# Gate and value products of the last two token groups in seven half-size products instead of eight

## The chip, the cores and the metric

The kernel runs on one core of one Trainium2 chip. The metric is the device time of one execution in microseconds (us); three runs of the kernel before gave 333.61, 334.01 and 334.57 us, median 334.01 us. The profile is one more execution of the same kernel, and it took 332.81 us.

## What is computed

Attention with a sliding window of 128 and a linear distance bias feeds a gated feed-forward block.

```python
scores = np.where(mask, scale * q @ k.T + bias, -1e9)      # 8 batches, 8 heads, 576 x 576, 64 deep
attn = softmax(scores) @ v                                  # 8 x 8 x 576 x 64
x = attn.transpose(0, 2, 1, 3).reshape(4608, 512)           # tokens x d_model
g = x @ w_gate                                              # 512 -> 1536
gelu = 0.5 * g * (1.0 + erf(g / sqrt(2)))
out = (gelu * (x @ w_val)) @ w_out                          # 1536 -> 512
```

## The kernel before, in words

**Groups and batches.** The 4608 tokens are worked through in nine groups `g` of 512. Attention of batch `g + 2` (scores, exponentials, masks, sums, products with v) is woven into the feed-forward work of group `g`, so that the last batch's attention is done in group 6 and groups 7 and 8 hold feed-forward work alone. The order of instructions on each engine is the order of the code; nothing is rescheduled. Each engine works through its own queue in that order and waits on semaphores for the others.

**Gate and value.** `gate_val(g, f)` (L631) makes one block `f` of 128 of the 1536 hidden columns: four matmuls of 128 x 512 into one PSUM bank for the gate and four into another for the value (L648; the contraction over 512 goes in four steps `c`). ScalarE then writes the GELU of the gate to `gelu` (L655), and VectorE multiplies the value bank with it into `hT` (L656). Twelve blocks make a group. PSUM has eight banks, handed out in turn by `bank()`, so matmuls run up to four blocks ahead of VectorE.

**Output products.** Groups 2 to 8 make the product with `w_out` in seven half-size products in place of eight (a Strassen-Winograd scheme): `combine_left` (L718) makes four sums of `hT` on VectorE, in three pieces at f = 7, 9 and 11, `product` (L739) makes the seven products in matmuls of 256 columns (L749), and `gather_out` (L756) copies and adds them from PSUM into `osb`. `out_products` (L1014) sets their order. For groups 7 and 8 it is the short list at L1018, for group 6 the branch at L1031, which also holds the last attention products.

**Around group 6.** At its beginning VectorE still has the last masks of batch 7 (L235) and the partial sums `T` of its weights to make (`add`, L385 to L395, run at f = 1 from `put_off`). They feed `sums4`, matmuls on `T` that stand behind block f = 4 in TensorE's queue (L438).

**Pool.** GpSimd issues the loads of q, k, v and the weights, sets a few tiles to zero, and has nothing to do after the load of v for batch 7 in group 5.

**Tiles that are free at the end.** `Ps[0]` (weights of even batches), `emask` (decay masks), `T`, `qT`, `kT` and `qs[0]` have no reader left in groups 7 and 8.

Of the kernel before, what the change touches and what calls it, by code (L numbers as in the profile page):

```python
# [7 lines left out]
FP32 = mybir.dt.float32  # L8
BF16 = mybir.dt.bfloat16
AF = mybir.ActivationFunctionType  # L10
ALU = mybir.AluOpType
# [10 lines left out]
COLUMNS0 = ((0, 192, 384), (None, None, 512, 704, 512))  # L22

RING = 2048

PRODUCTS = range(2, 9)

# [7 lines left out]
def kernel(  # L35
# [34 lines left out]
    def bank():  # L70
        return psum.tile([128, 512], FP32, name="ps")
# [51 lines left out]
    def load_v(b, js=range(5)):  # L123
        load(vb[b % 2], v, b, js, 64)
# [506 lines left out]
    def gate_val(g, f, lo=0, hi=512, later=None):  # L631
        if g not in hid:
            hid[g] = h_pool.tile([128, NF, 512], BF16, name="hT")
        t0 = 512 * g % RING
        n = hi - lo

        if n > 256 or lo >= 384:
            pg, pv = bank()[:, 0:n], bank()[:, 0:n]
            order = [(w, ps, c, c == 0) for w, ps in ((wg, pg), (wv, pv)) for c in range(4)]
        else:  # L640
            ps = bank()
            pg, pv = ps[:, 0:n], ps[:, n:2 * n]
            order = [(w, ps, c, w is wg and c == 0)
                     for cs in ((0, 1), (2, 3)) for w, ps in ((wg, pg), (wv, pv)) for c in cs]
        cols = ((0, 256), (256, 512)) if (g, f) in HALVED else ((0, n),)
        for w, ps, c, begins in order:
            for a, e in cols:
                nc.tensor.matmul(  # L648
                    out=ps[:, a:e], lhsT=w[:, c, 128 * f:128 * (f + 1)], rhs=xT[:, c, t0 + lo + a:t0 + lo + e],
                    start=begins and a == 0, stop=(c == 3),  # L650
                    skip_group_check=n <= 256 and lo < 384 or len(cols) > 1)

        def act():
            gl = g_pool.tile([128, 512], BF16, name="gelu")
            nc.scalar.activation(out=gl[:, 0:n], in_=pg, func=AF.Gelu)  # L655
            nc.vector.tensor_tensor(out=hid[g][:, f, lo:hi], in0=pv, in1=gl[:, 0:n],  # L656
                                    op=ALU.mult)

        if later is None:
            act()  # L660
        else:
            later.append(act)
# [10 lines left out]
    def store():  # L673
        for args in stores:
            nc.sync.dma_start(**args)
        stores.clear()
# [41 lines left out]
    def combine_left(g, lo, hi):  # L718
        x, ns = halves(g), slice(lo, hi)
        a11, a12, a21, a22 = (x[:, ns, e, h, :] for h in (0, 1) for e in (0, 1))  # L720
        s1, s2, s4 = (left[:, n, ns, :] for n in range(3))
        for to, a, b, op in ((s1, a21, a22, ALU.add), (s2, s1, a11, ALU.subtract),
                             (s4, a12, s2, ALU.subtract), (a21, a11, a21, ALU.subtract)):
            nc.vector.tensor_tensor(out=to, in0=a, in1=b, op=op)
# [14 lines left out]
    def product(g, n, a):  # L739
# [6 lines left out]
        for i in range(NF // 2):  # L746
# [2 lines left out]
            nc.tensor.matmul(out=made[g, a, into], lhsT=lhsT, rhs=rhs, start=first and i == 0,  # L749
                             stop=i == NF // 2 - 1, skip_group_check=True)  # L750

    def finished(g, t, osb):
        r0 = 512 * g + 128 * t
        stores.append(dict(out=out[r0:r0 + 128, :], in_=osb))
# [259 lines left out]
    def out_products(g):  # L1014
        b = g + 2
        O = lambda what, a, copy=act: gather_out(g, a, what, copy)
        P = lambda n, a: product(g, n, a)
        if b > B:  # L1018
            for n, after in ((1, ("p1",)), (2, ()), (6, ("u2", "c11")), (5, ("p5",)), (7, ("c22",)), (4, ("c21",)),
                             (3, ("c12",))):  # L1020
                for a in (0, 1):
                    P(n, a)
                    for what in after:
                        O(what, a)
                store()
            return
        P(1, 0)
        P(2, 0)
        O("p1", 0)
        urgent = 512 * (g + 2) - S * (b - 1)  # L1030
        if b == B:  # L1031
            P(6, 0)
            O("u2", 0)
            O("c11", 0)
            P(5, 0)
            O("p5", 0)
            P(7, 0)
            O("c22", 0)
            scale = values(b - 1, later=True)
            P(4, 0)  # L1040
            O("c21", 0)
            P(3, 0)
            scale[0]()
            scale[1]()
            O("c12", 0)
            P(1, 1)
            O("p1", 1)
            store()
            P(2, 1)
            for do in scale[2:]:  # L1050
                do()
            O("c11", 1)
            P(6, 1)
            O("u2", 1)
            P(5, 1)
            O("p5", 1)
            P(7, 1)
            O("c22", 1)
            P(3, 1)
            O("c12", 1)  # L1060
            P(4, 1)
            O("c21", 1)
            return
        exp_table()
        O("c11", 0)
        later = []
        scores2(b, 0, later)
        A = later[0]
        P(6, 0)
        O("u2", 0, dve)  # L1070
        P(5, 0)
        for n in (0, 1, 3):
            A[n]()
        O("p5", 0)
        A[2]()
        P(7, 0)
        O("c22", 0)
        A[4]()
        for n in (5, 6, 7):
            A[n]()  # L1080
        P(1, 1)
        P(4, 0)
        P(3, 0)
        O("p1", 1)
        O("c21", 0)
        O("c12", 0)
        A[8]()
        A[9]()
        scores2(b, 2, later)
        A = later[1]  # L1090
        P(2, 1)
        P(6, 1)
        O("u2", 1, dve)
        O("c11", 1)
        add(b, 0, None, (0,))
        P(5, 1)
        for n in (0, 1, 3, 5):
            A[n]()
        O("p5", 1)
        A[2]()  # L1100
        P(7, 1)
        O("c22", 1)
        A[4]()
        for n in (6, 7):
            A[n]()
        store()
        scale, more = values(b - 1, urgent=urgent)
        for do in scale:
            do()
        P(4, 1)  # L1110
        P(3, 1)
        O("c21", 1)
        for do in more:
            do()
        O("c12", 1)
        A[8]()
        A[9]()
        add(b, 0, None, (2, 1))
        put_off.append(lambda: add(b, 2))
# [3 lines left out]
    for g in range(NG):  # L1123
        if 1 <= g < B - 2:
            transposes_dma(3 if g == 1 else g + 2)
        if g == 1:

            nc.gpsimd.tensor_copy(out=mark, in_=kT[1][0:1, 0, 512:514])
            load_qk(4)
            load_v(3)  # L1130
        for f in range(9 if g == 0 else 0, NF):
            gate_val(g, f)
            if f == 1:
                for do in put_off:
                    do()
                put_off.clear()
                store()
            if g == 1 and f in (3, 5, 7, 9):
                combine_right(f // 2 - 1)
            if g in PRODUCTS and f in (7, 9, 11):  # L1140
                combine_left(g, *{7: (0, 3), 9: (3, 5), 11: (5, 6)}[f])
            if g == 2 and f == 2:
                add(3, 2, act, (1,))
            if g == 0 and f == 10:
                masks_of_last_blocks(0, 8)
            if g == 0 and f == 9:
                for c in range(4):
                    for w in (0, 1):
                        transpose(1, w, c, (act, dve)[w])
            if 2 <= g < B - 1:  # L1150
                if f == (5 if g == 2 else 4):
                    sums4(g + 1)
                if f == (7 if g == 2 else 6):
                    gather(g + 1)
                if f == (9 if g == 2 else 8):
                    spread_dma(g + 1)
                if f == 9 and g + 2 < B:

                    nc.gpsimd.tensor_copy(out=mark, in_=hid[g][0:1, f, 0:2])  # L1159
                    if g + 3 < B:  # L1160
                        load_qk(g + 3)
                    load_v(g + 2)
        if g == 0:
            nc.gpsimd.memset(Ps[0][:, :, 0:64], 0.0)
            for t in (qs[1], ks[1]):
                nc.gpsimd.memset(t[64:128, 4, :], 0.0)
        if g in PRODUCTS:
            out_products(g)
        else:
            for item in steps(g):  # L1170
                if isinstance(item, int):
                    out_part(g, item)
                else:
                    RUN[item[0]](*item[1:])
            store()
        if g == 0:
            load_v(2)
            nc.gpsimd.tensor_copy(out=mark, in_=qT[0][0:1, 0, 512:514])
            load_qk(3)
# [30 lines left out]
```

## Time and profile before

| | us |
|---|---|
| median of three runs | 334.01 |
| profiled execution | 332.81 |
| its span, first to last instruction | 331.0 |
| TensorE busy | 321.9 (97%) |
| VectorE busy | 244.2 (74%) |
| ScalarE busy | 174.7 (53%) |
| GpSimd busy | 109.5 (33%) |

The 1.8 us between the profiled execution and its span lie outside the instructions. In the profile PE is TensorE's matmuls, PEld its weight loads, DVE is VectorE, ACT ScalarE, POOL GpSimd. The granted TensorE clock is 1.0 throughout. A group of instructions is named by line, engine, operation and tiles, with its count, its busy time in us, the mean of one in ns, and the idle time of the engine just before it.

### The profile page before, as it was taken

The numbers are of one execution on the slowest core, as the hardware profiler recorded it, in microseconds if no ns is written. First come the engines' busy times: TensorE is split into PE (matmuls) and PEld (weight loads), VectorE is DVE, ScalarE is ACT, GpSimd is POOL, SyncE is SP. The second block draws the span as 40 slices with busy tenths as digits, with TensorE's granted clock in tenths as the row PEclk, the third lists the DMA queues.
The fourth block names the chain that finished last, engine by engine and source line by source line (L and its number), as shares of the span: only waits on it lengthen the run. The fifth ranks groups of instructions, "written<-read, shape, count | busy, mean of one in ns | idle before, by whom it ended". The sixth has DMA issues, their size and how long they took to land.

```text
span 331.0 us, 8767 instructions
## 1 busy us (share of the span) xinstructions
PE 321.9 (97%) x3513; PEld 192.7 (58%) x3544; DVE 244.2 (74%) x505; ACT 174.7 (53%) x341; POOL 109.5 (33%) x144
## 2 busy tenths in 40 slices
PE   8999999999999999999999999999999999999995
PEld 6566655544654477446844685458544854584474
DVE  8888776465779978978798879896997643933662
ACT  8974687537798276336643484338423233323331
POOL 5964789190292095007700690040000000000000
PEclk9999999999999999999999999999999999999999
DMA  8999999999799999949994999489105210011003
GB/s 218 170 197 189 204 168 183 131 220 146 158 155 142 142 199 193 152 115 200 185 144 111 180 192 152 129 159 119 69 1 135 73 69 0 2 61 68 0 0 128
DMA packets 149629, 43.53 MB, mean 131 GB/s; under 512 B 133556, under 2 KB 142420, under 8 KB 149588
## 3 DMA queue, kind: packets, MB, share of 16 engines
q0 software_dynamic: 107456, 18.10, 75.6%
q1 hardware_dynamic: 38960, 18.69, 26.0%
q10 hardware_dynamic: 3172, 6.19, 8.0%
q8 instruction: 27, 0.44, 0.6%
q14 instruction: 14, 0.11, 0.1%
HBM read 43.65 MB, written 9.53 MB: 161 GB/s over the span
## 4 chain that ended last, share of the span: by engine, by line
PE 93%; ACT 2%; DMA 1%; issue 1%; DVE 1%; SPq 0%
PE ps L648 56%; PE ps L749 19%; PE ps L502 5%; PE ps L685 5%; PE ps L301 2%; ACT P L232 2%; PE ps L705 2%; PE ps L219 1%; DMA qs<-in_q_dram 1%; PE ps L438 1%; PE ps L157 1%; ACT osb L769 0%; SPq L807 0%; DVE qT L165 0%; ACT rb L599 0%
## 5 line engine op out<-in xcount | busy, mean ns | idle before, releaser
L655 ACT ACTIVATE gelu<-ps 128x512 bf16<-128x512 f32 (+3 forms) x117 | 65.6, 564 | 107.4 <-PE ps L648 98.8
L648 PE MATMUL ps<-xT,wv 128*128 128x512 bf16 (+4 forms) x467 | 112.3, 361 | 0.3
L648 PE MATMUL ps<-xT,wg 128*128 128x512 bf16 (+4 forms) x454 | 110.9, 360 | 1.1 <-issue 0.3
L656 DVE TENSOR_TENSOR hT<-ps,gelu 128x512 bf16<-128x512 f32 (+3 forms) x117 | 73.3, 644 | 41.6 <-PE ps L648 36.5
L648 PEld LDWEIGHTS <-wv 128*128 128x128 bf16 x472 | 45.0, 98 | 48.8 <-DVE xT L556 0.6
L648 PEld LDWEIGHTS <-wg 128*128 128x128 bf16 x472 | 44.4, 98 | 46.4
L232 ACT ACTIVATE P<-ps 128x512 bf16<-128x512 f32 (+1 forms) x108 | 52.3, 575 | 4.0 <-PE ps L301 2.1
L235 DVE TENSOR_TENSOR P<-P,emask 128x768 bf16<-128x768 bf16 x60 | 32.0, 554 | 8.1 <-ACT P L232 6.3
L749 PEld LDWEIGHTS <-hT 128*128 128x128 bf16 x336 | 32.0, 97 | 6.4
L115 POOL DMA_DIRECT2D vb<-in_v_dram x40 | 33.9, 887 | 2.9 <-DMA wo<-in_moe_w_out_dram 1.0
L1159 POOL COPY mark<-hT 1x2 bf16<-1x2 bf16 x4 | 1.5, 366 | 77.8 <-DVE hT L656 77.8
L749 PEld LDWEIGHTS <-left 128*128 128x128 bf16 x252 | 24.3, 98 | 3.0
L115 POOL DMA_DIRECT2D qs<-in_q_dram x30 | 25.2, 857 | 1.8 <-issue 0.9
L115 POOL DMA_DIRECT2D ks<-in_k_dram x30 | 25.4, 889 | 0.3 <-DMA qs<-in_q_dram 0.3
L749 PE MATMUL ps<-right,hT 128*128 128x256 bf16 x168 | 22.1, 272 | 0.0
L749 PE MATMUL ps<-wo,hT 128*128 128x256 bf16 x168 | 21.0, 273 | 0.0
L749 PE MATMUL ps<-right,left 128*128 128x256 bf16 x168 | 20.3, 273 | 0.0
L502 PE MATMUL ps<-P,vb 64*64 64x192 bf16 (+2 forms) x752 | 18.5, 221 | 1.4 <-ACT P L232 0.7
L502 PEld LDWEIGHTS <-vb 64*64 64x64 bf16 x752 | 15.0, 107 | 4.3 <-issue 3.3
L685 PE MATMUL ps<-wo,hT 128*128 128x512 bf16 x66 | 15.9, 380 | 0.7 <-issue 0.6
L773 ACT COPY osb<-ps 128x256 f32<-128x256 f32 x14 | 5.6, 399 | 16.0 <-PE ps L749 16.0
L385 DVE TENSOR_TENSOR T<-P 64x1024 bf16<-64x1024 bf16 x20 | 13.7, 683 | 0.3
(111 smaller groups left out, 313.7 us busy)
## 6 DMA issues: line engine op xcount, KB each, us to landing
out_dram<-osb SPq DMA_DIRECT2D x36, 256.0 KB
rb<-rd ACTq DMA_DIRECT2D x10, 576.0 KB
vb<-in_v_dram POOLq DMA_DIRECT2D x32, 128.0 KB, 6.7
qs<-in_q_dram POOLq DMA_DIRECT2D x24, 128.0 KB, 5.1
ks<-in_k_dram POOLq DMA_DIRECT2D x24, 128.0 KB, 6.1
wo<-in_moe_w_out_dram POOLq DMA_DIRECT2D x4, 384.0 KB, 12.1
wg<-in_moe_w_gate_dram POOLq DMA_DIRECT2D x5, 256.0 KB, 8.6
wv<-in_moe_w_val_dram POOLq DMA_DIRECT2D x5, 256.0 KB, 9.6
```

Source lines behind the costliest of these rows:

```text
L115: nc.gpsimd.dma_start(out=t[at:at + n, j, :].rearrange("p (h d) -> p h d", h=H), in_=src[b][:, 128 * j:128 * j + n, :].rearrange("h p d -> ...
L232: nc.scalar.activation(out=dst, in_=src, func=AF.Exp, scale=0.125)
L235: nc.vector.tensor_tensor(out=dst, in0=dst, in1=m, op=ALU.mult)
L301: mm = nc.tensor.matmul(out=ps[64 * x:64 * x + 64, col:col + w], lhsT=keys(b, c, m)[half, :], rhs=qT[b % 2][half, c, q0:q0 + w], start=Tru ...
L385: nc.vector.tensor_tensor(out=to[half, :, x:x + 7:2], in0=P[half, :, 0:10:3], in1=P[half, :, 1:11:3], op=ALU.add)
L502: mm = nc.tensor.matmul(out=out, lhsT=lhsT, rhs=prob(b)[half, c, i, col:col + q1 - q0], start=all(t[2] != u for t in todo[:n]), stop=True, ...
L648: nc.tensor.matmul(out=ps[:, a:e], lhsT=w[:, c, 128 * f:128 * (f + 1)], rhs=xT[:, c, t0 + lo + a:t0 + lo + e], start=begins and a == 0, st ...
L655: nc.scalar.activation(out=gl[:, 0:n], in_=pg, func=AF.Gelu)
L656: nc.vector.tensor_tensor(out=hid[g][:, f, lo:hi], in0=pv, in1=gl[:, 0:n], op=ALU.mult)
L685: nc.tensor.matmul(out=acc[g], lhsT=hid[g][:, f, 128 * t:128 * (t + 1)], rhs=wo[:, f, :], start=(f == 0), stop=(f == NF - 1))
L705: nc.tensor.matmul(out=acc[g, t], lhsT=hid[g][:, f, 128 * t:128 * (t + 1)], rhs=wo[:, f, :], start=(f == 0), stop=(f == NF - 1))
L749: nc.tensor.matmul(out=made[g, a, into], lhsT=lhsT, rhs=rhs, start=first and i == 0, stop=i == NF // 2 - 1, skip_group_check=True)
```

## The change

In groups 7 and 8 the blocks f = 0 to 3 and f = 6 to 9 are no longer made by `gate_val`. `gate_quad` makes four blocks at a time. It takes gate and value weights as the two rows of a 2 x 2 block matrix and the two halves of the contraction as its columns; the other factor has the two halves of the contraction as rows and the two halves of 256 tokens as columns. The product of the two comes in seven products, each of eight matmuls of 256 columns (two output banks `u`, two blocks `e`, two steps `c`). Blocks 4, 5, 10 and 11 stay with `gate_val`.

The sums that go into it are new. `combine_weights` makes four sums of weights for each of the two places, 16 additions of 128 x 512 on GpSimd, at the beginning of group 6, into `Ps[0]` and `emask`. `combine_x` makes four sums of tokens of a group, 128 x 512 each, on VectorE, into `T`: for group 7 at the end of group 6, for group 8 behind block 4 of group 7. What comes out of it is new too: P1, U = P1 + P6 and P5 are copied from PSUM to float32 tiles (`wide`), five copies on ScalarE and one on VectorE; six additions on VectorE add a PSUM bank to them; four GELUs read those tiles; VectorE multiplies the first half of the tokens (two operations), GpSimd the second half (two). The pieces of `combine_left` move from f = 7, 9, 11 to f = 4, 5, 10, 11.

```diff
+    def combine_weights():
+        for f0, at in QUADS.items():
+            for c in (0, 1):
...
+                for to, a, b, op in ((s1, v1, v2, ALU.add), (s2, s1, g1, ALU.subtract),
+                                     (s3, g1, v1, ALU.subtract), (s4, g2, s2, ALU.subtract)):
+                    nc.gpsimd.tensor_tensor(out=to, in0=a, in1=b, op=op)
...
+        factors = {1: (g1, b11), 2: (g2, b21), 3: (s4, b22), 4: (v2, t4), 5: (s1, t1), 6: (s2, t2), 7: (s3, t3)}
...
+        P(1)
+        for u in (0, 1):
+            copy(out=P1[u], in_=banks["x", u])
+        P(2)
+        for u in (0, 1):
+            add_to("z", P1, u)
+        gelu(0, P1, 0)
+        P(6)
+        copy(out=U[0], in_=banks["x", 0])
+        dve(out=U[1], in_=banks["x", 1])
+        P(5)
+        for u in (0, 1):
+            copy(out=P5[u], in_=banks["y", u])
+        gelu(0, P1, 1)
+        P(7)
+        for u in (0, 1):
+            add_to("x", P5, u)
+        P(3)
+        for u in (0, 1):
+            add_to("y", U, u)
+            gelu(1, U, u)
+        P(4)
+        for u in (0, 1):
+            nc.vector.tensor_tensor(out=hidden(u, 0), in0=both(banks["x", u]), in1=both(gelus[u]), op=ALU.mult)
+            nc.gpsimd.tensor_tensor(out=hidden(u, 1), in0=both(P5[u]), in1=both(gelus[2 + u]), op=ALU.mult)
...
+            combine_x(g + 1)                      # end of out_products, group 6
...
+        if g == B - 2:
+            combine_weights()
+        if g >= B - 1:
+            for f in range(NF):
+                if f in QUADS:
+                    gate_quad(g, f)
+                elif not any(f0 < f < f0 + 4 for f0 in QUADS):
+                    gate_val(g, f)
+                if f == 4:
+                    store()
+                    combine_left(g, 0, 2)
+                    if g + 1 < NG:
+                        combine_x(g + 1)
+                if f in (5, 10, 11):
+                    combine_left(g, *{5: (2, 3), 10: (3, 5), 11: (5, 6)}[f])
+            out_products(g)
+            continue
```

Two places of the queues, in the order of instructions. A name in brackets is an engine whose semaphore the instruction waits for; DVE in an instruction of DVE is an earlier result of its own. First VectorE's queue before, from the first block of group 7 on: `hT<-ps,gelu` is the multiplication of a block, `left` and `hT<-hT` are `combine_left`.

```order
L656 TENSOR_TENSOR hT<-ps,gelu 128x512 [waits DVE_49,PE_49,Activation_49]
L656 TENSOR_TENSOR hT<-ps,gelu 128x512 [waits PE_49,Activation_49] x7
L724 TENSOR_TENSOR left<-hT 128x768 [waits DVE_49]
L724 TENSOR_TENSOR left<-left,hT 128x768 [waits DVE_49]
L724 TENSOR_TENSOR left<-hT,left 128x768 [waits DVE_49]
L724 TENSOR_TENSOR hT<-hT 128x3x256
L656 TENSOR_TENSOR hT<-ps,gelu 128x512 [waits PE_49,Activation_49] x2
```

The same queue after, in the first four blocks of group 7, behind the four operations of `combine_x`: `qT_99` holds P1, `kT_101` U and `qT_100` P5; `qs_95` holds the GELUs.

```order
L816 TENSOR_TENSOR qT_99<-ps,qT_99 128x512 [waits PE_49,Activation_49] x2
L836 COPY kT_101<-ps 128x512 [waits PE_49]
L816 TENSOR_TENSOR qT_100<-ps,qT_100 128x512 [waits PE_49,Activation_49] x2
L816 TENSOR_TENSOR kT_101<-ps,kT_101 128x512 [waits PE_49,Activation_49]
L816 TENSOR_TENSOR kT_101<-ps,kT_101 128x512 [waits DVE_49,PE_49]
L850 TENSOR_TENSOR hT<-ps,qs_95 128x2x256 [waits DMASW1_49,PE_49]
L850 TENSOR_TENSOR hT<-ps,qs_95 128x2x256 [waits DMASW2_49,PE_49,Activation_49]
L658 TENSOR_TENSOR hT<-ps,gelu 128x512 [waits PE_49,Activation_49]
L726 TENSOR_TENSOR left<-hT 128x512 [waits Pool_49]
L726 TENSOR_TENSOR left<-left,hT 128x512 [waits DVE_49]
L726 TENSOR_TENSOR left<-hT,left 128x512 [waits DVE_49]
L726 TENSOR_TENSOR hT<-hT 128x2x256
```

Four blocks took four operations of VectorE and take nine, and the first piece of `combine_left` now waits for Pool. Behind it in the queue stand the four operations of `combine_x` for group 8, the multiplication of block 5, and the next piece of `combine_left`.

The second place is the end of Pool's queue. Before, it ends with the load of v for batch 7 in group 5:

```order
L1159 COPY mark<-hT 1x2
L115 DMA vb_104<-in_v_dram 128x8x64 x4
L115 DMA vb_104<-in_v_dram 64x8x64
L1205 UNCONDITIONAL_BRANCH
L1205 ISA
```

After, the sums of weights stand behind that load (`P_105` is `Ps[0]`):

```order
L1278 COPY mark<-hT 1x2
L117 DMA vb_104<-in_v_dram 128x8x64 x4
L117 DMA vb_104<-in_v_dram 64x8x64
L768 TENSOR_TENSOR P_105<-wv 128x512
L768 TENSOR_TENSOR P_105<-P_105,wg 128x512
L768 TENSOR_TENSOR P_105<-wg,wv 128x512
L768 TENSOR_TENSOR emask<-wg,P_105 128x512
L768 TENSOR_TENSOR P_105<-wv 128x512
L768 TENSOR_TENSOR P_105<-P_105,wg 128x512
L768 TENSOR_TENSOR P_105<-wg,wv 128x512
L768 TENSOR_TENSOR emask<-wg,P_105 128x512
```

Eight more of the same follow, and then eight multiplications into `hT`, two for each four blocks. The first sum waits for the last reader of `Ps[0]`, the products of batch 6 with v in group 5.

More of the change, by code (lines that the diff above doesn't have):

```diff
@@ L24 @@
 RING = 2048
+QUADS = {0: 0, 6: 512}
 PRODUCTS = range(2, 9)
@@ L750, in product, with flat_of @@
                              stop=i == NF // 2 - 1, skip_group_check=True)
+    def flat_of(t):
+        return t.rearrange("p a x -> p (a x)")
+    sums_w = [flat_of(t)[:, lo:lo + 2048].rearrange("p (c f) -> p c f", c=2)
+              for t, lo in ((Ps[0], 0), (Ps[0], 2048), (Ps[0], 4096), (emask, 0))]
+    def combine_weights():
+        for f0, at in QUADS.items():
+            for c in (0, 1):
+                g1, g2, v1, v2 = (w[:, x, 128 * f0:128 * f0 + 512]
+                                  for w, x in ((wg, c), (wg, 2 + c), (wv, c), (wv, 2 + c)))
+                s1, s2, s3, s4 = (t[:, c, at:at + 512] for t in sums_w)
+                for to, a, b, op in ((s1, v1, v2, ALU.add), (s2, s1, g1, ALU.subtract),
+                                     (s3, g1, v1, ALU.subtract), (s4, g2, s2, ALU.subtract)):
+                    nc.gpsimd.tensor_tensor(out=to, in0=a, in1=b, op=op)
@@ new lines, in sums_x, with tokens, combine_x @@
+    def sums_x(g):
+        return [flat_of(T)[:, 2048 * (g % 2) + 512 * n:2048 * (g % 2) + 512 * n + 512].rearrange(
+            "p (c x) -> p c x", c=2) for n in range(4)]
+    def tokens(g):
+        t0 = 512 * g % RING
+        return [xT[:, c:c + 2, t0 + x:t0 + x + 256] for c in (0, 2) for x in (0, 256)]
+    def combine_x(g):
+        b11, b12, b21, b22 = tokens(g)
+        t1, t2, t3, t4 = sums_x(g)
+        for to, a, b, op in ((t1, b12, b11, ALU.subtract), (t2, b22, t1, ALU.subtract),
+                             (t3, b22, b12, ALU.subtract), (t4, b21, t2, ALU.subtract)):
+            nc.vector.tensor_tensor(out=to, in0=a, in1=b, op=op)
@@ new lines, with gate_quad, P, add_to @@
+    wide = [flat_of(t)[:, 1024 * i:1024 * i + 1024].bitcast(FP32)
+            for t in (qT[0], kT[0], qT[1]) for i in (0, 1)]
+    gelus = [flat_of(qs[0])[:, 512 * i:512 * i + 512] for i in range(4)]
+    def gate_quad(g, f0):
+        if g not in hid:
+            hid[g] = h_pool.tile([128, NF, 512], BF16, name="hT")
+        b11, b12, b21, b22 = tokens(g)
+        t1, t2, t3, t4 = sums_x(g)
+        s1, s2, s3, s4 = (t[:, :, QUADS[f0]:QUADS[f0] + 512] for t in sums_w)
+        g1, g2, v1, v2 = (w[:, c:c + 2, 128 * f0:128 * f0 + 512] for w in (wg, wv) for c in (0, 2))
+        factors = {1: (g1, b11), 2: (g2, b21), 3: (s4, b22), 4: (v2, t4), 5: (s1, t1), 6: (s2, t2), 7: (s3, t3)}
+        banks = {}
+        def P(n):
+            w, x = factors[n]
+            for u in (0, 1):
+                if n in (1, 2, 5):
+                    banks[INTO[n], u] = bank()
+                ps = banks[INTO[n], u]
+                for e in (0, 1):
+                    at = 256 * u + 128 * e
+                    for c in (0, 1):
+                        nc.tensor.matmul(
+                            out=ps[:, 256 * e:256 * e + 256], lhsT=w[:, c, at:at + 128], rhs=x[:, c, :],
+                            start=n in (1, 2, 5) and e == 0 and c == 0, stop=c == 1, skip_group_check=True)
+        copy, dve = nc.scalar.copy, nc.vector.tensor_copy
+        P1, U, P5 = wide[0:2], wide[2:4], wide[4:6]
+        def add_to(n, to, u):
+            nc.vector.tensor_tensor(out=to[u], in0=banks[n, u], in1=to[u], op=ALU.add)
+        def gelu(what, frm, u):
+            nc.scalar.activation(out=gelus[2 * what + u], in_=frm[u], func=AF.Gelu)
+        def both(x):
+            return x.rearrange("p (e x) -> p e x", e=2)
+        def hidden(u, half):
+            return hid[g][:, f0 + 2 * u:f0 + 2 * u + 2, 256 * half:256 * half + 256]
+        P(1)
[20 more added lines that the diff above has]
+        P(4)
+        for u in (0, 1):
+            nc.vector.tensor_tensor(out=hidden(u, 0), in0=both(banks["x", u]), in1=both(gelus[u]), op=ALU.mult)
+            nc.gpsimd.tensor_tensor(out=hidden(u, 1), in0=both(P5[u]), in1=both(gelus[2 + u]), op=ALU.mult)
```

## Prediction

> **What bounds the kernel now.** First the page: how much of the span TensorE is busy.
>
> ```profile
> span 331.0 us, 8767 instructions
> PE 321.9 (97%) x3513; PEld 192.7 (58%) x3544; DVE 244.2 (74%) x505; ACT 174.7 (53%) x341; POOL 109.5 (33%) x144
> ```
>
> Then the chain of waits over the end of the program, columns start, us, what. It begins here with group 8.
>
> ```profile
> 297.34 10.74 PE ps L648 x49
> 308.07 0.05 issue
> 308.13 9.88 PE ps L648 x45
> 318.00 9.26 PE ps L749 x84
> 327.26 0.02 issue
> 327.29 0.42 DVE osb L776
> ```
>
> Nothing but matmuls stands in it: whatever shortens TensorE's queue in groups 7 and 8 shortens the time, and whatever makes it wait lengthens it. Group 8's gate and value matmuls run from 297.34 to 318.00, 20.66 us for 12 x 8 = 96 matmuls of 512 columns (two records are missing), 0.215 us each. The 84 matmuls of 256 columns behind them take 9.26 us, 0.110 us each, a little over half. Then the busy time in two stretches of group 7, columns length, PE, PEld, DVE, ACT, POOL:
>
> ```profile
> 270.00:280.00 10.00, 9.95 (x47) 4.57 (x47) 3.95 (x6) 3.52 (x6) 0.00 (x0) 1.00 0.00 0
> 280.00:290.00 10.00, 10.00 (x58) 5.44 (x56) 8.20 (x18) 3.73 (x7) 0.00 (x0) 1.00 0.01 2
> ```
>
> VectorE has room where blocks stand alone (3.95 of 10 us) and little where `combine_left` is added (8.20 of 10).
>
> **The matmuls.** Four blocks take 32 matmuls of 512 columns, 32 x 0.215 = 6.89 us; now 7 x 8 = 56 of 256 columns, 56 x 0.110 = 6.17 us. That is 0.71 us, four times, **2.86 us saved**.
>
> **What VectorE and ScalarE get instead.** The groups by shape from 225 us to the end give the prices: busy, mean ns, idle before.
>
> ```profile
> L656 DVE TENSOR_TENSOR hT<-ps,gelu 128x512 bf16<-128x512 f32 x36 | 24.5, 688 | 20.8 <-PE ps L648 20.6
> L655 ACT ACTIVATE gelu<-ps 128x512 bf16<-128x512 f32 x36 | 21.5, 597 | 40.1 <-PE ps L648 40.1
> L765 DVE COPY osb<-ps 128x256 f32<-128x256 f32 x2 | 0.8, 425 | 1.5 <-PE ps L749 1.5
> L767 DVE TENSOR_TENSOR osb<-ps,osb 128x256 f32<-128x256 f32 x7 | 2.9, 421 | 0.6 <-PE ps L749 0.5
> ```
>
> An addition of float32 and a copy from PSUM take the same 0.42 us for 256 columns, and a multiplication of 512 columns, with a bf16 operand, takes 0.69. That is 0.27 us for 256 columns more, or 1 ns each, so I give the new additions and the copy of 512 columns 0.69 us too. How closely such operations follow each other, and how long they wait for a matmul, is read from the timeline:
>
> ```profile
> 243.37 1.89 DVE L656 TENSOR_TENSOR hT<-ps,gelu 128x512 bf16<-128x512 f32 x3
> 315.38 0.43 DVE L724 TENSOR_TENSOR left<-hT 128x512 bf16<-128x512 bf16 x1
> 315.84 0.42 DVE L724 TENSOR_TENSOR left<-left,hT 128x512 bf16<-128x512 bf16 x1
> 316.30 0.43 DVE L724 TENSOR_TENSOR left<-hT,left 128x512 bf16<-128x512 bf16 x1
> 316.64 0.42 DVE L724 TENSOR_TENSOR hT<-hT 128x512 bf16<-128x512 bf16 x1
> 316.98 0.68 DVE L656 TENSOR_TENSOR hT<-ps,gelu 128x512 bf16<-128x512 f32 x1
> 317.84 2.78 PE L749 MATMUL ps<-wo,hT 128*128 128x256 bf16 x24
> 318.11 0.69 DVE L656 TENSOR_TENSOR hT<-ps,gelu 128x512 bf16<-128x512 f32 x1 [0.45 <-PE ps L648]
> 318.69 0.37 ACT L763 COPY osb<-ps 128x256 f32<-128x256 f32 x1 [0.92 <-PE ps L749]
> 318.84 0.29 DVE L724 TENSOR_TENSOR left<-hT 128x256 bf16<-128x256 bf16 x1
> 319.70 0.28 DVE L724 TENSOR_TENSOR hT<-hT 128x256 bf16<-128x256 bf16 x1
> ```
>
> Multiplications in a row stand 0.63 us apart. A set of four bf16 sums of 512 columns takes 1.60 us (315.38 to 316.98), one of 256 columns 1.07 us (318.84 to 319.70, and 0.21). VectorE starts 0.27 us after the last matmul of a bank is issued (317.84 to 318.11), ScalarE 0.19 us after (12 matmuls end at 318.50, copy at 318.69). Between VectorE and ScalarE I take 0.06 us, an estimate from the same handovers without the matmul's way.
>
> Now the queue of group 7, t = 0 at its first product, each product 0.88 us. `combine_x` for group 7 stands behind group 6 on VectorE and is over by 1.4 us, when P2 ends: hidden. VectorE then has two additions (P2), one copy (P6), two additions (P7), two (P3): the last ends at 6.84. GELUs of the second half follow at 6.26 and 6.90; VectorE's two multiplications and block 4's end at 8.85, which is near where TensorE is. Pool starts its first multiplication when the first of those GELUs ends, at 6.92, and its second behind it.
>
> No operation of Pool that reads two tiles is in the trace. The nearest row is a memory fill of the same size, which only writes:
>
> ```profile
> L1164 POOL MEMSET P<- 128x512 bf16 x1 | 0.5, 530 | 0.0
> ```
>
> One stream takes 0.53 us, so 0.53 is the lower bound and three streams in turn, 1.59 us, the upper; I take two, reads in turn with the write beside them, **1.06 us**, the middle. The Trainium skill's page "GPSIMD Engine Reference", section 3.1, measures 4.50 us for an addition of 2048 float32, a quarter of which is 1.12 us as an estimate; the sum by that would be 0.4 us more.
>
> So Pool is done at 6.92 + 2 x 1.06 = 9.04, and the first piece of `combine_left` starts on VectorE at 9.10. Queued behind it: 1.60 for that piece, 1.48 for `combine_x` of group 8 (its third sum needn't wait), 0.64 for block 5, 1.07 for the second piece. The first addition of the second four blocks starts at 13.9. TensorE, unhindered, has issued P1, P2, P6 and P5 of these by 9.63 + 3.53 = 13.16, and P7 goes into the bank that holds U, so it waits for U's copies: on ScalarE behind a GELU, which waits for that addition (13.90 + 0.69, GELU 0.52, copy 0.60), on VectorE behind both additions. P7 starts at 15.83: **2.67 us lost**. In group 8 `combine_x` is not there, VectorE is 1.48 us earlier, and the same wait is **1.19 us**. First four blocks of each group: no wait. Blocks 10 and 11: VectorE reaches block 11's product at 23.0, done at 23.7, just when the last matmul of P2 needs it (23.80): nothing, but 0.1 us of Pool more would show, in each group.
>
> With Pool at 0.53 us VectorE and not Pool is late, and the two waits are 2.37 and 0.89; at 1.59 they are 3.73 and 2.25, and P2 waits 1.0 more in each group, 7.9 in all. So the sum is 2.86 saved, less 3.86 (3.26 to 7.9): 1.0 us longer (0.4 to 5.1). For the profiled execution that is 333.8 us; the median lies 1.2 us above it (334.01 to 332.81), so **335.0 us** (334.4 to 339.1).
>
> At nothing I cost three edits, by two rows of the chain:
>
> ```profile
> 232.45 1.13 PE ps L502 x51
> 267.37 10.74 PE ps L648 x49
> ```
>
> They are `combine_weights` in its place, 16 x 1.06 = 17 us of Pool, from 233.6 (where batch 6's products have read `Ps[0]`) to 251, needed in group 7 from 267.4 on; the moved `store()`, since output tiles have been stored before they are wanted; and the copies on ScalarE, nine operations in 6.17 us at 0.6.
>
> **Rivals.** *First, slower by far:* Pool's sums of weights hold up VectorE in group 6. What the profile says of a tie between the two engines:
>
> ```profile
> 97.16 3.58 POOL L115 DMA_DIRECT2D vb<-in_v_dram  x4
> 99.35 0.76 DVE L395 COPY T<-P 64x1024 bf16<-64x1024 bf16 x1
> L395 DVE COPY T<-P x18: 357/418/797, 99.4 to 243.0; 64x1024 bf16<-64x1024 bf16 x9, 64x768 bf16<-64x768 bf16 x9
> L385 DVE TENSOR_TENSOR T<-P 64x1024 bf16<-64x1024 bf16 x18 | 12.3, 683 | 0.3
> L385 DVE TENSOR_TENSOR T<-P 64x1024 bf16<-64x1024 bf16 x2 | 1.4, 681 | 0.0
> ```
>
> A copy that takes 0.418 us alone took 0.76 beside a load that Pool issues. The additions L385 took 0.683 us from 90 to 235 us, with such loads about, and 0.681 from 235 to 262 without: Pool's loads don't touch them. Whether a sum on Pool does, no row shows. The place where it would count:
>
> ```profile
> 237.12 1.02 DVE L235 TENSOR_TENSOR P<-P,emask 128x768 bf16<-128x768 bf16 x2
> 242.53 0.81 DVE L395 COPY T<-P 64x1024 bf16<-64x1024 bf16 x2
> 243.56 0.68 PE L438 MATMUL ps<-T,ones 128*32 128x128 bf16 x32
> ```
>
> From 237.12 to 243.34 VectorE has twelve operations on SBUF alone (two masks, four sums and six copies of `T`), and TensorE's `sums4` starts 0.22 us after the last. If each waits once for a sum on Pool, it is up to 12 x 1.06 - 0.2 = 12.5 us; with Pool at 0.53 only about nine sums are left by then, 4.8 us. On top of the forecast: 340 to 347.5 us, decided by whether a Pool sum keeps VectorE from SBUF for its whole length. The Trainium skill's page "SBUF — State Buffer", section "Who interferes with whom", states it so: an operation of VectorE with two inputs in SBUF contends with one of GpSimd that reads SBUF, and whichever comes second is blocked for the whole instruction. The constant 683 ns agrees with its other half, that the loads, which write only, don't hurt such sums. I give this 0.32.
>
> *Second, faster:* VectorE's queue is shorter than I add up, the additions of two float32 at less than 0.69 us and Pool near its lower bound, so that both waits shrink below 1.9 us together. With neither wait the time is 334.0 - 2.9 = 331.1, with half of the two 333.1. For it speaks that VectorE idles before every block in the row of L656 (20.8 us over 36), against it that its sum over the first six blocks is 12.5 us of work beside 13.2 of matmuls, with a wait for Pool amid it. 0.17.
>
> *Third,* the matmuls don't get shorter, because 56 weight loads in place of 32 bind: at 0.110 us for 84 of the same form they don't, and PEld is busy 58%. With the waits it would be 337.9; 0.03.
>
> **The numbers.** A measurement of this kernel tells a change of about 0.3%, 1.0 us, from none. The forecast of 335.0 has 0.48, and lies at that bound: same 0.20, slower 0.25, faster 0.03. First rival, all slower: 0.32. Second: faster 0.15, same 0.02. Third: counted half slower, half the same as if its waits were shorter, 0.015 each. Sums: faster 0.18, same 0.235, slower 0.585. Range: the forecast's own is 334.4 to 339.1; below it the second rival reaches in to 332.3, above it the first to 345.0, with about one in ten left out on each side.
>
> **What would show it.** Right: seven products per four blocks with 56 matmuls at 0.11 us; the waits of TensorE in groups 7 and 8 before P7 of the second four blocks, about 2.7 and 1.2 us, with ScalarE's copy as the releaser; `combine_left` at f = 4 waiting for Pool; group 6 as long as before. Wrong: `sums4` or blocks 4 to 8 of group 6 later on TensorE and VectorE's sums of `T` stretched (first rival); no wait before P7 (second); Pool's multiplications far from 1.06 us, which moves each of the waits by twice the difference.

## The result, and the profile after

The changed kernel takes 348.32 us (median of six runs, 348.07 to 348.63) against 334.24 us before (six runs, 332.82 to 336.07): a ratio of 1.0427 (95% interval 1.0407 to 1.0448), 4% slower. The forecast was 335.0 us with a range up to 345.0. The profiled execution took 348.32 us with a span of 346.5, 15.5 us longer than before.

The page, its busy times and TensorE's granted clock in 40 slices:

```profile
span 346.5 us, 9094 instructions
PE 326.9 (94%) x3640; PEld 204.3 (59%) x3640; DVE 268.5 (77%) x541; ACT 184.6 (53%) x361; POOL 138.9 (40%) x168
PEclk9999999999999999999999999999859999899999
```

TensorE is busy 94% instead of 97%, and its clock falls to half in two places, from 249.0 to 259.3 us and from 296.8 to 300.2 us by the trace. The timeline of the first of them, start, duration, engine, operation, and in brackets the idle time before and who ended it:

```profile
237.62 1.98 DVE L237 TENSOR_TENSOR P<-P,emask 128x768 bf16<-128x768 bf16 x2
239.52 1.17 DVE L391 COPY T<-P 64x256 bf16<-64x256 bf16 x1
240.69 1.15 POOL L768 TENSOR_TENSOR P<-P,wg 128x512 bf16<-128x512 bf16 x1
240.70 1.29 DVE L392 TENSOR_TENSOR T<-P 64x256 bf16<-64x256 bf16 x1
245.75 3.10 DVE L387 TENSOR_TENSOR T<-P 64x1024 bf16<-64x1024 bf16 x2
251.13 2.57 DVE L397 COPY T<-P 64x1024 bf16<-64x1024 bf16 x2
252.53 0.29 PE L440 MATMUL ps<-T,ones 128*32 128x128 bf16 x2 [7.03 <-DVE T L397]
253.76 1.12 PE L440 MATMUL ps<-T,ones 128*32 128x128 bf16 x29 [0.94 <-DVE T L397]
254.81 1.89 PE L650 MATMUL ps<-xT,wg 128*128 128x512 bf16 x4
256.49 1.91 PE L650 MATMUL ps<-xT,wv 128*128 128x512 bf16 x4
259.59 1.03 PE L650 MATMUL ps<-xT,wv 128*128 128x512 bf16 x4
```

This is group 6. The kernel before had at the same place, beside the masks and copies that the prediction shows:

```profile
238.06 0.21 DVE L389 COPY T<-P 64x256 bf16<-64x256 bf16 x1
238.28 0.29 DVE L390 TENSOR_TENSOR T<-P 64x256 bf16<-64x256 bf16 x1
240.61 1.38 DVE L385 TENSOR_TENSOR T<-P 64x1024 bf16<-64x1024 bf16 x2
```

Two masks that took 1.02 us take 1.98, a copy of 0.21 us takes 1.17, a sum of 0.29 us takes 1.29, two sums of 1.38 us take 3.10. The sum of 0.29 us starts together with a sum on Pool and ends 0.15 us behind it. The twelve operations from the masks to the last copy into `T` take 14.85 us in place of 5.01, 0.82 us more each, and `sums4` (L440) waits for them. Then the products behind it run at half speed, 1.9 us for four matmuls instead of 1.03. The second place is group 7:

```profile
286.80 2.27 POOL L851 TENSOR_TENSOR hT<-qT,qs 128x512 bf16<-128x512 f32 x2 [32.08 <-ACT qs L819]
289.10 0.43 DVE L726 TENSOR_TENSOR left<-hT 128x512 bf16<-128x512 bf16 x1 [0.33 <-POOL hT L851]
293.95 1.28 DVE L816 TENSOR_TENSOR qT<-ps,qT 128x512 f32<-128x512 f32 x2
295.20 0.57 ACT L835 COPY kT<-ps 128x512 f32<-128x512 f32 x1
295.82 1.03 PE L808 MATMUL ps<-T,P 128*128 128x256 bf16 x8 [2.63 <-ACT kT L835]
296.69 1.79 PE L808 MATMUL ps<-xT,emask 128*128 128x256 bf16 x8
298.27 1.91 PE L808 MATMUL ps<-T,wv 128*128 128x256 bf16 x8
300.97 1.03 PE L650 MATMUL ps<-xT,wv 128*128 128x512 bf16 x4
327.25 1.03 PE L808 MATMUL ps<-T,P 128*128 128x256 bf16 x8 [1.22 <-ACT kT L835]
```

`combine_left` waits for Pool, VectorE comes to the first addition of the second four blocks at 293.95, ScalarE's copy of U is done at 295.77, and P7 starts 2.63 us late. In group 8 it is 1.22 us late (last row). Behind the wait of 2.63 us the clock falls too; behind that of 1.22 it doesn't.

Where the 15.5 us went, by the starts of the same matmuls in both traces: 0.5 us lies ahead of group 6, where nothing was changed (executions differ there by up to 2 us). From group 6's first gate matmul to its first output product it is 33.75 us against 21.44, 12.3 more: 9.1 of them waits of TensorE (1.16, 7.03 and 0.94), and 3.2 in `sums4` and the blocks behind it, at half the clock. From there to the last addition it is 73.74 against 71.02, 2.7 more: 2.86 saved, 2.63 and 1.22 lost in waits, and 1.65 in the products between 295.82 and 300.97, which need 3.5 us at the full clock.

### The profile page after: what moved, and what is told of

The parts are those of the page before. It is cut to its first block, busy times and chain, and to the rows that moved or that the text cites. A ratio compares the mean times of both kernels' runs of the same rounds, so it can differ in the third digit from the quotient of the medians.

```text
span 346.5 us, 9094 instructions
## 1 busy us (share of the span) xinstructions
PE 326.9 (94%) x3640; PEld 204.3 (59%) x3640; DVE 268.5 (77%) x541; ACT 184.6 (53%) x361; POOL 138.9 (40%) x168
## 4 chain that ended last, share of the span: by engine, by line
PE 86%; DVE 7%; ACT 3%; issue 3%; POOL 1%; ACTq 0%; DVEq 0%
PE ps L650 43%; PE ps L751 18%; PE ps L808 6%; PE ps L687 5%; PE ps L504 5%; PE ps L303 2%; PE ps L221 2%; PE ps L707 2%; ACT P L234 2%; PE ps L78 1%; DVE T L397 1%; PE ps L440 1%; DVE xT L558 1%; POOL hT L851 1%; DVE P L237 1%
## 5 line engine op out<-in xcount | busy, mean ns | idle before, releaser
L657 ACT ACTIVATE gelu<-ps 128x512 bf16<-128x512 f32 (+3 forms) x101 | 56.0, 559 | 98.3 <-PE ps L650 83.5
L650 PE MATMUL ps<-xT,wg 128*128 128x512 bf16 (+4 forms) x408 | 98.0, 363 | 0.0
L650 PE MATMUL ps<-xT,wv 128*128 128x512 bf16 (+4 forms) x408 | 97.3, 361 | 0.0
L658 DVE TENSOR_TENSOR hT<-ps,gelu 128x512 bf16<-128x512 f32 (+3 forms) x101 | 62.3, 637 | 26.9 <-PE ps L650 21.9
L650 PEld LDWEIGHTS <-wv 128*128 128x128 bf16 x408 | 39.0, 98 | 41.9 <-issue 1.3
L650 PEld LDWEIGHTS <-wg 128*128 128x128 bf16 x408 | 38.5, 99 | 39.7 <-issue 2.1
L237 DVE TENSOR_TENSOR P<-P,emask 128x768 bf16<-128x768 bf16 x60 | 33.0, 571 | 8.3 <-ACT P L234 6.5
L851 POOL TENSOR_TENSOR hT<-qT,qs 128x512 bf16<-128x512 f32 x8 | 9.1, 1157 | 69.1 <-ACT qs L819 69.1
L687 PE MATMUL ps<-wo,hT 128*128 128x512 bf16 x72 | 16.9, 380 | 0.0
L387 DVE TENSOR_TENSOR T<-P 64x1024 bf16<-64x1024 bf16 x20 | 15.4, 768 | 0.3
```

The costliest lines, as they stand in the source:

```text
L237: nc.vector.tensor_tensor(out=dst, in0=dst, in1=m, op=ALU.mult)
L387: nc.vector.tensor_tensor(out=to[half, :, x:x + 7:2], in0=P[half, :, 0:10:3], in1=P[half, :, 1:11:3], op=ALU.add)
L650: nc.tensor.matmul(out=ps[:, a:e], lhsT=w[:, c, 128 * f:128 * (f + 1)], rhs=xT[:, c, t0 + lo + a:t0 + lo + e], start=begins and a == 0, st ...
L687: nc.tensor.matmul(out=acc[g], lhsT=hid[g][:, f, 128 * t:128 * (t + 1)], rhs=wo[:, f, :], start=(f == 0), stop=(f == NF - 1))
L851: nc.gpsimd.tensor_tensor(out=hidden(u, 1), in0=both(P5[u]), in1=both(gelus[2 + u]), op=ALU.mult)
```

## The experiments

Theory A: a sum on Pool and an operation of VectorE whose operands all lie in SBUF keep each other out for a whole instruction, and that is the loss in group 6, with the clock's fall behind it. The loss in groups 7 and 8 is VectorE's queue, as forecast. Each run is compared with the kernel before on the same chip; in the first four it took 334.0 us (11 runs), in the last four 334.08 (17 runs).

**The sums alone** (kernel before, with `combine_weights` and its tiles)

```diff
+        if g == B - 2:
+            combine_weights()
         for f in range(9 if g == 0 else 0, NF):
             gate_val(g, f)
```

> The kernel before with the 16 sums of weights on Pool added at the place where the change has them; nothing reads them, gate and value products are as before. Theory A (a sum on Pool and an operation of VectorE with all its operands in SBUF keep each other out for their whole length): the twelve such operations of VectorE from 237 to 243 us take 1.0 to 1.5 us each in place of 0.2 to 0.7, sums4 on TensorE comes about 9 us later, the granted clock falls behind that wait, and the time is 12 to 12.8 us above the kernel before, about 346.7. Theory B (the wait in group 6 comes from the new products and their buffers, the sums are hidden): within 1 us of the kernel before.

345.88 us, ratio 1.0362 (1.0333 to 1.0391). The timeline of group 6:

```profile
238.55 1.98 DVE L237 TENSOR_TENSOR P<-P,emask 128x768 bf16<-128x768 bf16 x2
246.68 3.11 DVE L387 TENSOR_TENSOR T<-P 64x1024 bf16<-64x1024 bf16 x2
253.47 0.29 PE L440 MATMUL ps<-T,ones 128*32 128x128 bf16 x2 [7.03 <-DVE T L397]
```

The same masks, the same sums and the same wait as in the changed kernel, without one of its new products. 11.9 us are lost by sums that nothing reads. Theory B falls.

**Fills in place of the sums**

```diff
-                    nc.gpsimd.tensor_tensor(out=to, in0=a, in1=b, op=op)
+                    for _ in range(2):
+                        nc.gpsimd.memset(to, 0.0)
```

> The changed kernel with each of the 16 sums of weights replaced by two fills of the same tile with zero on Pool (the products that read the sums get zeros, so this part of the result is left out). Pool is busy about as long at the same place, 32 x 0.53 = 17 us, but reads nothing. Theory A, if the tie is in reading: VectorE's masks and sums there are as in the kernel before (0.55 and 0.68 us), its six copies of T stretch somewhat, as they do beside Pool's loads; group 6 loses 0 to 3 us and the time is 336.5 to 340. Theory A', any work of Pool in SBUF keeps VectorE out: each of the twelve operations waits for a fill of 0.53 us, some 5 to 8 us, 342 to 346.

336.53 us, ratio 1.0082 (1.0050 to 1.0114). Its timeline at the same place:

```profile
237.41 1.02 DVE L237 TENSOR_TENSOR P<-P,emask 128x768 bf16<-128x768 bf16 x2
237.71 3.64 POOL L769 MEMSET P<- 128x512 bf16 x6
238.34 0.54 DVE L391 COPY T<-P 64x256 bf16<-64x256 bf16 x1
238.90 0.29 DVE L392 TENSOR_TENSOR T<-P 64x256 bf16<-64x256 bf16 x1
241.54 1.38 DVE L387 TENSOR_TENSOR T<-P 64x1024 bf16<-64x1024 bf16 x2
```

Pool is as busy, but it only writes: VectorE's masks and sums take what they took before (1.02, 0.29, 1.38), and only copies are longer (0.54 for 0.21). So Pool's writing alone doesn't keep VectorE's sums out; what the fills leave out is its reading. The copies are held up by Pool's writing as well.

**The sums at other times** (a small copy on Pool holds each piece back until VectorE has written what it reads)

```diff
+    def combine_weights(n, behind=None):
+        if behind is not None:
+            nc.gpsimd.tensor_copy(out=mark, in_=behind)
+        for _ in range(n):
+            nc.gpsimd.tensor_tensor(**weights_left.pop(0))
...
-            combine_weights()
+            combine_weights(3)
...
+            if g == B - 2 and f == 2:
+                combine_weights(6, hid[g][0:1, 2, 0:2])
+            if g == B - 2 and f == 11:
+                combine_weights(7, left[0:1, 2, 5, 0:2])
```

> The changed kernel with the 16 sums of weights in three pieces, held back by small copies on Pool that wait for a result of VectorE: three at once, six behind block 2 of group 6 (when the sums of T are done), seven behind the last piece of combine_left of group 6. The same work on Pool, but beside operations of VectorE that read PSUM. Theory A: group 6 is as in the kernel before, the whole loss there is gone, 12.3 us: 336.0 (335.3 to 337.5), what is left being the 2.7 us that groups 7 and 8 lose. A rival, that the sums cost TensorE by being in the program at all (code, semaphores, reads of wg and wv): 344 or more.

336.28 us, ratio 1.0071 (1.0048 to 1.0095). The timeline, with one place where the two still meet:

```profile
238.60 1.02 DVE L237 TENSOR_TENSOR P<-P,emask 128x768 bf16<-128x768 bf16 x2
242.09 1.38 DVE L387 TENSOR_TENSOR T<-P 64x1024 bf16<-64x1024 bf16 x2
245.04 0.68 PE L440 MATMUL ps<-T,ones 128*32 128x128 bf16 x32
251.43 1.15 POOL L776 TENSOR_TENSOR P<-wv 128x512 bf16<-128x512 bf16 x1
251.73 1.27 DVE L726 TENSOR_TENSOR left<-hT 128x768 bf16<-128x768 bf16 x1
```

The same sixteen sums cost nothing when VectorE reads PSUM beside them: from group 6's first gate matmul to its first output product it is 21.44 us, as in the kernel before. Where the last of the second piece meets `combine_left`, one operation waits until Pool is done (1.27 us for 0.55), and nothing comes of it, since it had time.

**The sums of tokens later** (changed kernel; the added lines stand in the loop of `out_products` for groups 7 and 8)

```diff
-                    if g + 1 < NG:
-                        combine_x(g + 1)
...
+                if n == 6 and g + 1 < NG:
+                    combine_x(g + 1)
```

> The changed kernel with the four sums of tokens of group 8 moved from behind block 4 of group 7 into its output products (behind P6), where VectorE is idle. Theory A (the wait before P7 in group 7 is VectorE's queue, 1.5 us of which are these four sums, and a wait of 2.6 us costs another 1.6 us by a clock that falls to half behind it, while a wait of 1.2 us does not): P7's wait in group 7 is 1.2 us, the clock stays, the time falls by 3.0 us to 345.3. Rival C (the clock's fall has another cause than this wait): it falls by 1.4 us, to 346.9. Rival D (ScalarE's queue or Pool sets the wait): no change.

345.55 us, ratio 1.0345 (1.0320 to 1.0371), 2.8 us less than the changed kernel. TensorE's waits before P7 in groups 7 and 8:

```profile
295.33 1.03 PE L808 MATMUL ps<-T,P 128*128 128x256 bf16 x8 [1.17 <-ACT kT L835]
325.16 1.03 PE L808 MATMUL ps<-T,P 128*128 128x256 bf16 x8 [1.23 <-ACT kT L835]
```

The wait in group 7 falls from 2.63 to 1.17, the products behind it take 1.03 us again, and the time falls by both. All four executions have a mean granted clock of 0.985, where the six of the changed kernel have 0.980: the second fall is gone, the one in group 6 is still there.

**Something to do while TensorE waits** (changed kernel)

```diff
     def sums4(b):
         ps = bank()
+        if b == 7:
+            keep_busy(ps, 130, 128)
```

> The changed kernel with 130 small matmuls of zeros (128 columns) ahead of sums4 in group 6, into the bank that sums4 then overwrites: TensorE has something to do while it waits for VectorE there. Theory A (of the 12.3 us lost in group 6 some 9.1 are the wait and the rest, 2.2 in the next gate and value products and some 0.9 in sums4 itself, is the clock that falls to half behind it): the wait for VectorE stays, the granted clock stays at 1.0 there, the time falls by 2.2 to 3.1 us, to 345.6. Rival E (the slow products behind sums4 have another cause, such as VectorE's backlog): no gain, 348, or a loss.

345.54 us, ratio 1.0367 (1.0328 to 1.0407), by the medians 2.8 us less than the changed kernel, although TensorE has 130 matmuls more. The four executions spread from 344.24 to 348.26 us, with mean granted clocks from 1.0 to 0.99, so the size of the gain is read from the profile, which is of the shortest, at 1.0:

```profile
245.37 7.42 PE L78 MATMUL ps<-zeros 128*128 128x128 bf16 x130 [1.16 <-DVE hT L660]
253.87 0.66 PE L442 MATMUL ps<-T,ones 128*32 128x128 bf16 x29 [0.91 <-DVE T L397]
254.46 1.04 PE L652 MATMUL ps<-xT,wg 128*128 128x512 bf16 x4
293.30 1.03 PE L810 MATMUL ps<-T,P 128*128 128x256 bf16 x8 [2.63 <-ACT kT L837]
294.17 1.04 PE L810 MATMUL ps<-xT,emask 128*128 128x256 bf16 x8
```

`sums4` comes as late as before (253.87, 253.76 in the changed kernel), but it and the blocks behind it run at the full clock: from group 6's first gate matmul to its first output product it is 31.14 us against 33.75, 2.6 less.

The last two rows show something that the edit doesn't touch. TensorE waits 2.63 us before P7 in group 7, as in the changed kernel, and here no fall of the clock follows. From group 6's first output product to the last addition it is therefore 72.15 us against 73.74. These 1.6 us are luck of this execution, and a wait of 2.63 us is not always followed by a fall.

**Half of the sums** (as the sums alone, with the eight for the first four blocks only)

```diff
-        for f0, at in QUADS.items():
+        for f0, at in list(QUADS.items())[:1]:
```

> The kernel before with only the first 8 of the 16 sums on Pool, at the same place; nothing reads them. Theory A, counted operation by operation: three sums run while VectorE reads PSUM, the other five each keep back one of the twelve operations of VectorE by about 1 us, and the rest of the twelve run as in the kernel before. sums4 comes 4.5 to 5 us later, the clock behind it costs 1.5 to 2.5, together 6 to 7 us: 340.5. Rival F (the loss isn't per operation, any stream of sums there makes VectorE's whole stretch slow): 10 us or more. Rival G (a buffer of slack takes up short delays): under 3 us.

340.17 us, ratio 1.0180 (1.0153 to 1.0206). The timeline:

```profile
239.74 2.90 DVE L237 TENSOR_TENSOR P<-P,emask 128x768 bf16<-128x768 bf16 x2
243.74 1.17 DVE L392 TENSOR_TENSOR T<-P 64x256 bf16<-64x256 bf16 x1
244.92 0.79 DVE L397 COPY T<-P 64x1024 bf16<-64x1024 bf16 x2
249.34 1.51 PE L440 MATMUL ps<-T,ones 128*32 128x128 bf16 x31 [2.64 <-DVE T L397]
250.78 1.89 PE L650 MATMUL ps<-xT,wg 128*128 128x512 bf16 x4
```

While there are sums on Pool, each operation of VectorE waits (the masks take 2.90 us, the sum 1.17); from the first one behind them on they take what they took before (0.79). The loss is by the operation. TensorE's wait is 2.64 us in place of 7.03, and behind it, too, four matmuls take 1.89 us in place of 1.03.

**Both edits together** (the sums at other times, and the sums of tokens later)

```diff
-            combine_weights()
+            combine_weights(3)
...
-                    if g + 1 < NG:
-                        combine_x(g + 1)
```

> The changed kernel with the sums of weights in three pieces apart from VectorE's work in SBUF, and the sums of tokens of group 8 in group 7's output products. Theory A: group 6 loses nothing, the waits before P7 are 1.2 us in each of groups 7 and 8 with the clock at 1.0; 2.86 us saved less 2.4 lost is 0.4 us below the kernel before: 333.8 (333.0 to 334.6), no difference that can be measured. If the two edits work on the same loss: 336.

333.40 us, ratio 0.9985 (0.9969 to 1.0002): no difference from the kernel before that can be told, as the sum of 2.86 saved and 2.4 lost says.

**The copies of U first** (on top of both)

```diff
         P(6)
-        copy(out=U[0], in_=banks["x", 0])
-        dve(out=U[1], in_=banks["x", 1])
+        for u in (0, 1):
+            copy(out=U[u], in_=banks["x", u])
         P(5)
         for u in (0, 1):
             copy(out=P5[u], in_=banks["y", u])
+        gelu(0, P1, 0)
         gelu(0, P1, 1)
```

(`gelu(0, P1, 0)` ahead of `P(6)` goes.)

> The same as the run with both apart, and in each set of four blocks ScalarE makes both copies of U, ahead of the two GELUs of the first half of the tokens (which move behind the copies of P5). P7 then waits for nothing that stands in VectorE's queue. Theory A: no wait before P7 in either group, all of the 2.86 us is kept: 331.4 (331.0 to 332.5), faster than the kernel before by 0.8%. Rival H (the wait moves on, to P4, which needs VectorE's additions to P5, or to the output products, which need combine_left): 332.5 to 334.5.

330.98 us, ratio 0.9909 (0.9890 to 0.9927): 0.9% faster than the kernel before. The chain of waits in group 7; group 8's rows have the same lengths, but 9.33 in the last:

```profile
269.02 6.11 PE ps L816 x56
275.13 3.45 PE ps L650 x16
278.58 6.11 PE ps L816 x56
284.70 3.45 PE ps L650 x16
288.15 9.31 PE ps L751 x84
```

Matmuls follow each other without a wait: 56 matmuls in 6.11 us for each four blocks, where the forecast had 6.17. On ScalarE a GELU had stood ahead of a copy that TensorE waits for, and on VectorE two additions ahead of the other copy, while the GELU itself is first read behind P4.

## Why the prediction was wrong

The step that failed is the one that costs `combine_weights` in its place at nothing; it cost 11.9 us by itself in the run with the sums alone. Its working looked at when Pool's sums would be done (251 us; they were done at 254.7), and not at what VectorE does beside them. The mechanism stood as the first rival, with 0.32, and it is the one that came; I had let the likeliest case be the one without a row against it. The row was missing because no operation of Pool in the kernel before reads two tiles: the constant 683 ns of VectorE's sums is from beside Pool's loads, and beside the fills, which only write, those sums were unchanged too. The Trainium skill's page "SBUF — State Buffer", section "Who interferes with whom", says that a VectorE operation with two inputs in SBUF contends with a GpSimd operation that reads SBUF; these runs agree, with 0.76 us more for each of the six masks and sums. The six copies, which have one input, took 0.88 us more each, and the fills held them up as well.

What that rival's price lacked was the clock. It put the wait at up to 12.5 us, with each operation waiting for a whole sum; TensorE waited 9.1. But behind the wait 3.2 us more were lost, of which keeping TensorE busy gave 2.6 back. The same term is missing in group 7, 1.65 us behind the wait of 2.63, and it put the time beyond the rival's upper end of 347.5.

The other steps held. The saving for four blocks, forecast at 0.71 us, is 0.78: 6.11 us in the last run against 6.89. The waits before P7 were forecast at 2.67 and 1.19 us and measured 2.63 and 1.22. That VectorE's queue makes them was shown by moving `combine_x`, which took the first to 1.17; of Pool's part the trace shows 0.33 us, the time that `combine_left` waits for it, and no run tried it alone. Pool's multiplications take 1.16 us, with a forecast of 1.06 (0.53 to 1.59); the quarter from the Trainium skill's page "GPSIMD Engine Reference", section 3.1, an estimate of 1.12, was nearer. With the sums at other times, so without the loss in group 6, the changed kernel takes 336.28, 1.3 above the forecast. The clock accounts for it: six of the eight executions have a mean granted clock of 0.995, which is one fall (median 336.69), and two have 1.0 (334.46 and 335.68).

Two readings were off, with little weight in the sum. The matmuls that end at 318.50 are six and not twelve (6 x 0.110 = 0.66 us from 317.84), and multiplications in a row start 0.60 us apart and not 0.63, since the 1.89 us for three end with the 0.69 us of the last.

The second rival (a shorter queue) fell for the kernel as it was: both waits were there. The third fell: 56 weight loads don't bind.

## What to carry to other kernels

Work that is moved to an idle engine is not hidden by that engine's idleness: ask what it shares with the engines that are busy at that time, and put it where those read elsewhere, here beside VectorE's reads of PSUM. A wait of TensorE can have a price beyond its length, so a wait of a few us should be priced with the half-speed products that can follow it, as an upper bound. And of the instructions ahead of the one that TensorE waits for, ask of each whether its result is needed as soon: in each set of four blocks, one GELU moved behind the copies, and one copy taken from VectorE's queue, were together worth 2.4 us (333.40 to 330.98).

## What the runs showed of the hardware

- Sums on Pool hold up VectorE's sums in SBUF, and also the other way: in the changed kernel the first sum on Pool took 1.58 us, where a mask started beside it, and the third 1.15 us, beside an addition that reads PSUM. Fills on Pool held up only VectorE's copies in SBUF (0.54 us for 0.21).
- Behind a wait of TensorE of 2.63 to 2.65 us the granted clock fell to half for 3.41 us in four profiles (the changed kernel, the fills, the sums at other times, half of the sums). Behind the same 2.63 us in the kept-busy profile it didn't, nor behind waits of 1.16 to 1.24 us. The Trainium skill's page "TensorE: Matmul & The Clock Gate", part 1, gives one idle window of about 3.4 us as the condition for half the clock; here a shorter wait was enough.
- Where the wait lies seems to decide. In the clock records of each trace the changes lie whole multiples of 3.413 us apart; the two falls of the changed kernel start at 249.02 and 296.81 us, 14 such steps. Counted on these steps, the wait before P7 lies with 2.42 us in one step in the changed kernel, and wholly in one with the fills and with the sums at other times, and the clock falls at the end of that step. In the kept-busy profile it is split into 1.79 and 0.84 us, and the clock stays. This is worked out from the traces; no run shifted a wait in order to test it.
